# A new step list for a windowed attention with four experts behind it, on one core

## The chip, the cores and the metric

The kernel runs on one NeuronCore of a Trainium2 chip. The metric is device time in microseconds of one launch, as the median of several runs. Five runs of the kernel before lie between 232.1 and 235.28 us, with a median of 234.81 us.

## The reference

Inputs are q, k and v of shape (8 batches, 8 heads, 576 positions, 64), and weights of a gate (512 x 4), of four experts' projections (4 x 512 x 64 each for q, k and v) and of their outputs (4 x 64 x 512). All are float32. Cut to what is computed:

```python
scores = (q @ k.T) / 8, where |i - j| <= 32, else -1e9   # per batch and head
x = softmax(scores) @ v            # heads joined: (8, 576, 512)
logits = x @ w_gate                # 4 experts; the two largest are softmaxed to weights w
for e in range(4):
    qe, ke, ve = x @ wq[e], x @ wk[e], x @ wv[e]
    ye = causal_softmax(qe @ ke.T / 8) @ ve @ wo[e]
    out += w[:, e] * ye            # 0 for an expert that was not chosen
```

## The kernel before, in words

The program is straight-line code without loops at run time: 901 steps, one after another, as the string ORDER (lines 24 to 89) names them. Each name is an operation, its indices, and, behind an @, the PSUM banks and sometimes the engine. `ex0110@0` is operation ex for batch 0, head group 1, half 1, pair 0, from the bank pair that begins at 0; `xf10@6a` is operation xf for batch 1, part 0, bank 6, on ACT (a; v is DVE, g is POOL). The loop at line 680 calls the functions of these names. Each engine executes its own instructions in the order of this list; semaphores order engines against one another, only where tiles overlap. [...] a step cannot write a bank until whoever reads its former content is through. So the list sets the order on every engine, in SP's queue of transfers, and the use of every bank.

Per batch the steps are these.

- **Loads**: lq and lk bring q and k of four heads (576 KB each), lv brings V in pieces of 128 positions (256 KB; the last is 128 KB); fk and fq are the first batch's loads in halves; wl0 to wl3 bring the weights (512 KB each). All are issued by SP through `load`.
- **First attention**: tq and tk (gq and gk in the first batch) transpose 32 x 32 blocks on DVE. sc writes scores of four heads and half the positions to two bank pairs: 80 loads of weights and 80 matmuls in float32. ex takes their exponential on ACT into A, two steps for each sc. mk multiplies A by the window mask on POOL. vc copies V to make a second alignment. av multiplies A with V (32 matmuls; column 65 is the sum). un divides on DVE into XN.
- **Middle**: xt transposes XN on TensorE, xf copies it out of PSUM, xb casts it to bfloat16. ga computes the gate's logits, and gt, ge, gm, gu make weights of them on DVE and ACT. cw0 to cw3 cast the experts' weights, once.
- **Experts**: pp and pv project (8 matmuls, and 16 or 8), pe and ve copy these out, ps writes scores in four pieces, xe takes exponentials into ATE, se masks on POOL, po multiplies with V (30 matmuls), oe normalises and weights, ox transposes by DMA (pt and ot on TensorE in the last batch), py multiplies by WO, ye copies to Y and st stores it (pz, yz and sz in the last batch).

The steps that begin with s_ prepare constants; s_wm issues 30 matmuls on zeros while the first loads are under way.

Two mechanisms matter here. A load waits for the last TensorE instruction that stands before it in the list, in addition to what its buffer needs:

```python
ins = nc.sync.dma_start(o, i)
if PACE[0] is not None:
    tc.add_manual_dep(ins.ins, PACE[0].ins.name, AFTER, reason="pace")
```

So loads start where TensorE has got to, and SP's queue is in order: a load or store that waits holds those behind it. And the instructions of TensorE themselves come from memory, in blocks, while the program runs; the profile shows them as a queue of their own.

ORDER was written by a search (simulated annealing) that works on a model of the engines; the model isn't part of the kernel. One of its numbers is the time from the request of a block of TensorE instructions to its arrival.

## Time and profile before

| | us |
|---|---|
| median of five runs (lowest, highest) | 234.81 (232.1, 235.28) |
| profiled execution, whole | 236.81 |
| profiled execution, span from first to last instruction | 235.1 |
| TensorE: matmuls busy | 214.9 |
| TensorE: weight loads busy | 174.9 |
| DVE, ACT, POOL busy | 177.5, 155.2, 148.8 |
| mean granted TensorE clock | 0.955 |

In the profile PE is TensorE's matmuls, PEld its loads of weights, DVE is VectorE, ACT is ScalarE, POOL is GpSimd, SP is SyncE. Nearly all instructions carry the line of one helper (line 145), so they are told apart by tiles: "PS<-Tqn,Tkn" is a score step (sc), "PS<-V,A" an av step, "A<-PS" on ACT an ex, "A<-A,MASKP" on POOL a mk. The page divides the span into 40 slices of 5.9 us; its clock row gives tenths of full speed. The chain is the work that ended last, followed back; "issue" is time in which an engine waited for nothing that the profile shows. A median of 277 ns for one matmul is its length in a pipeline, not the distance to the next.

### The profile page before, as it was taken

How to read it: one execution, taken by the hardware profiler on the slowest of the kernel's cores; microseconds unless marked ns; L12 is line 12 of the kernel's file. 1: busy time of each engine (PE TensorE's matmuls, PEld its weight loads, DVE VectorE, ACT ScalarE, POOL GpSimd, SP SyncE). 2: the span in 40 equal slices, each digit the busy share in tenths (PEclk: the TensorE clock that was granted, in tenths of full speed). 3: DMA queues.
4: the chain of work that ended last, by engine and by line, in shares of the span. 5: the costliest groups of instructions: out<-in, count | busy, mean ns of one | idle time of the engine just before them, and what ended most of it. 6: DMA issues, size and time to landing. Idle time of an engine off the chain costs nothing.

```text
span 235.1 us, 12226 instructions
## 1 busy us (share of the span) xinstructions
PE 214.9 (91%) x5485; PEld 174.9 (74%) x5496; DVE 177.5 (75%) x359; ACT 155.2 (66%) x241; POOL 148.8 (63%) x166
## 2 busy tenths in 40 slices
PE   6777799989989989999999899999989999999992
PEld 5656697878779867877876788787888887876650
DVE  7987669987789858978985798877877926665571
ACT  2143319778873867638766767778836788886972
POOL 7089705979971989888699682587820898150220
PEclk9775569999999999999999999999999999999999
DMA  6989467958994589675739788887752554228346
GB/s 177 361 220 321 140 166 177 236 110 229 233 323 129 129 163 228 172 228 122 178 74 322 240 199 167 233 216 121 203 190 105 31 139 162 53 53 231 117 178 230
DMA packets 64533, 42.94 MB, mean 183 GB/s; under 512 B 54752, under 2 KB 55776, under 8 KB 64480
## 3 DMA queue, kind: packets, MB, share of 16 engines
q1 hardware_dynamic: 64400, 42.09, 67.7%
q8 instruction: 43, 0.70, 1.3%
q14 instruction: 10, 0.08, 0.1%
q10 hardware_dynamic: 80, 0.07, 0.1%
HBM read 30.42 MB, written 9.44 MB: 170 GB/s over the span
## 4 chain that ended last, share of the span: by engine, by line
PE 68%; DVE 11%; DMA 7%; issue 6%; ACT 5%; SPq 0%; ACTq 0%; DVEq 0%
PE PS L145 68%; DMA kn<-in_k_dram 5%; DVE Tkn L145 5%; ACT ATE L145 2%; DMA V<-in_v_dram 2%; DVE Tqn L145 1%; ACT V L145 1%; DVE OE L145 1%; DVE PS L145 1%; ACT A L145 1%; DVE XTF L145 1%; DVE VE L145 0%; ACT QKE L145 0%; DVE m L145 0%; ACT Y L145 0%
## 5 line engine op out<-in xcount | busy, mean ns | idle before, releaser
L145 POOL TENSOR_TENSOR A<-A,MASKP 128x576 f32<-128x576 f32 x64 | 89.4, 1417 | 20.6 <-ACT A L145 20.0
L145 ACT ACTIVATE A<-PS 128x576 f32<-128x576 f32 x64 | 38.6, 651 | 40.5 <-PE PS L145 40.3
L145 ACT ACTIVATE ATE<-PS 128x1024 bf16<-128x1024 f32 (+1 forms) x64 | 50.9, 837 | 15.5 <-PE PS L145 14.9
L145 PE MATMUL PS<-Tqn,Tkn 32*64 32x128 f32 (+2 forms) x2560 | 46.6, 277 | 7.5 <-issue 3.8
L145 PEld LDWEIGHTS PS<-Tqn,Tkn 32*64 32x64 f32 x2560 | 41.3, 141 | 13.4 <-issue 5.2
L145 PE MATMUL PS<-V,A 128*64 128x65 f32 (+1 forms) x1280 | 43.1, 234 | 3.0 <-issue 1.9
L145 PEld LDWEIGHTS PS<-V,A 128*64 128x64 f32 (+1 forms) x1280 | 39.5, 142 | 6.9 <-issue 4.1
L145 POOL TENSOR_SCALAR_AFFINE_SELECT ATE<-ATE 128x512 bf16<-128x512 bf16 (+1 forms) x48 | 24.3, 519 | 30.9 <-ACT ATE L145 30.6
L145 DVE STREAM_TRANSPOSE Tqn<-qn 128x576 f32<-128x576 f32 (+1 forms) x34 | 37.4, 1177 | 4.7 <-PE PS L145 2.5
L145 DVE STREAM_TRANSPOSE Tkn<-kn 128x576 f32<-128x576 f32 (+1 forms) x34 | 37.4, 1176 | 3.0 <-DMA kn<-in_k_dram 2.5
L145 DVE TENSOR_TENSOR XN<-PS,RC 128x512 f32<-128x512 f32 (+1 forms) x40 | 25.5, 638 | 1.4
L145 POOL CAST XTB<-XTF 128x128 bf16<-128x128 f32 (+1 forms) x20 | 13.9, 713 | 19.4 <-ACT XTF L145 12.5
L145 POOL COPY V<-V 64x1024 f32<-64x1024 f32 (+1 forms) x20 | 18.6, 931 | 4.1 <-DMA V<-in_v_dram 3.0
L145 PE MATMUL PS<-WO,OTT 128*128 128x512 bf16 (+1 forms) x85 | 18.8, 342 | 0.9 <-DVE G L145 0.3
L145 PE MATMUL PS<-ident,XN 128*128 128x128 f32 x144 | 19.0, 276 | 0.0
L145 PE MATMUL PS<-WV,XTB 128*128 128x256 bf16 (+1 forms) x192 | 18.5, 255 | 0.0
L145 PE MATMUL PS<-XTB,WQ 128*128 128x288 bf16 x128 | 18.2, 286 | 0.1
L145 PEld LDWEIGHTS <-ATE 128*128 128x128 bf16 x480 | 16.7, 97 | 2.1 <-issue 0.8
L145 PE MATMUL PS<-XTB,WK 128*128 128x288 bf16 x128 | 18.2, 286 | 0.0
L145 PE MATMUL PS<-QKE 64*128 64x64 bf16 (+4 forms) x192 | 16.7, 277 | 1.2 <-DVE QKE L145 0.9
L145 PE MATMUL PS<-VE,ATE 128*128 128x65 bf16 x480 | 17.4, 193 | 0.1
L145 PEld LDWEIGHTS PS<-ident,XN 128*128 128x128 f32 x144 | 16.0, 140 | 2.0 <-ACT ATE L145 0.2
(66 smaller groups left out, 241.2 us busy)
## 6 DMA issues: line engine op xcount, KB each, us to landing
qn<-in_q_dram SPq DMA_DIRECT2D x15, 576.0 KB, 5.6
kn<-in_k_dram SPq DMA_DIRECT2D x15, 576.0 KB, 5.3
V<-in_v_dram SPq DMA_DIRECT2D x32, 256.0 KB, 4.4
out_dram<-Y SPq DMA_DIRECT2D x14, 512.0 KB, 3.8
V<-in_v_dram SPq DMA_DIRECT2D x8, 128.0 KB, 3.6
out_dram<-Y SPq DMA_DIRECT2D x4, 256.0 KB, 2.7
out_dram<-YS SPq DMA_DIRECT2D x15, 64.0 KB, 2.8
kn<-in_k_dram SPq DMA_DIRECT2D x2, 288.0 KB, 4.0
```

The lines of the kernel that those rows point to most:

```text
L145: return lambda *a, **k: self._w.note(self._e, f(*a, **k))
```

## The change

Only the string ORDER is new. The search was run anew with a longer assumed time from the request to the arrival of each block of TensorE instructions. The new list has the same 901 step names. What differs is their order, the banks, and for some copies the engine. The beginning and the last steps, before (-) and after (+):

```diff
-    s_mask s_onev s_warm s_onep s_padx s_ident fk01 s_padv@v fq00 fk00 fq01 fq10 gk01 fk10 lq10 gq00 s_wm
-    gk00 lv03 gq01 sc000@02 ex0001@2 mk0001 gq10 lv02 sc001@46 gk10 lk10 lv01 ex0011@6 sc011@62 lv04 lv00
-    tq10 tk10 ex0111@2 mk0011 lq11 s_pada@v vc01@g ex0000@0 sc010@20 tq11 mk0111 mk0000 ex0010@4 mk0010
-    ex0110@6 mk0110 ex0100@2 lq20 lk11 sc101@64 ex0101@0 av02@0 ex1010@6 ex1011@4 vc00@a mk0101 mk0100 lk21
-    av03@6 un02@0 un03@6 wl0 av04@2 un04@2 mk1011 mk1010 av01@0 un01@0 av00@6 un00@6 lk20 sc100@24 wl1
-    ex1001@4 xt00@6 xf00@6a tk11 xt01@0 xt02@4 xf02@4a xf01@0a xb01@a sc111@64 ex1111@4 lv12 lv14 cw0@v tq20
+    s_padx s_onep fk00 fq00 gk00 s_mask fq01 fk01 fq10 fk10 lq10 gq00 s_wm gq01 gk01 lv03 gq10 sc001@02 lk10
+    sc000@46 gk10 lv04 s_warm ex0000@4 ex0010@0 ex0011@2 lv02 sc011@04 tq10 lv01 lq11 tk10 ex0111@4 sc010@24
+    lv00 ex0110@0 ex0001@6 mk0011 vc01@a ex0100@2 ex0101@4 lk11 s_pada@v s_onev tq11 sc101@60 mk0010
+    s_padv@g mk0000 mk0111 lq20 mk0110 av02@4 ex1011@0 lv12 sc100@02 un02@4 lv13 vc00@a mk0101 mk0001
+    s_ident mk0100 av03@4 lk20 ex1001@2 ex1010@6 ex1000@0 mk1011 mk1010 vc11@g tk11 un03@4 av00@0 un00@0 wl1
+    av01@6 xt01@0 xf01@0a wl0 av04@2 un01@6 xt00@6 un04@2 xt02@0 xf02@0v xb01@g xf00@6a xb00@a sc110@24
...
-    oe702@2 pt702@2 ot712@0a yz71@1a sz71 pz70@3 yz70@3a sz70 ot702@2v pz73@2 yz73@2a sz73 pz72@0 yz72@0v
-    sz72 py72@1 ye72@1a st72
+    pt702@0 oe712@6 ot702@0v pz71@1 yz71@1a sz71 pt712@2 pz70@3 yz70@3a sz70 ot712@2v pz72@2 yz72@2a sz72
+    pz73@0 yz73@0a sz73 py72@1 ye72@1a st72
```

Engines of copies that change: cw0, cw2 and cw3 go from DVE to ACT (cw1 stays on DVE); s_padv goes from DVE to POOL; of vc1 ACT has one in place of three, POOL seven in place of five, and of vc0 two and six in place of three and five; two xf0, one pe, two ye2 and one yz go from DVE to ACT; one ve0, one ve1 and one ot go from ACT to DVE, and one ye0. In the new list lv73 stands ahead of pv41, in the old one ahead of mk7001; lv74 stands behind st22, st32 and st20.

## The prediction

> **What bounds the kernel now.** I read the page's busy row and slices first, then the chain that ended last, then the waits, then stretches of 3.41 us at the start, because the clock row is low there.

> ```profile
> PE 214.9 (91%) x5485; PEld 174.9 (74%) x5496; DVE 177.5 (75%) x359; ACT 155.2 (66%) x241; POOL 148.8 (63%) x166
> ...
> PEclk9775569999999999999999999999999999999999
> DMA  6989467958994589675739788887752554228346
> ...
> q8 instruction: 43, 0.70, 1.3%
> ...
> PE 68%; DVE 11%; DMA 7%; issue 6%; ACT 5%; SPq 0%; ACTq 0%; DVEq 0%
> ```

> TensorE bounds: busy for 91%, and 68% of the chain. What can be won is its idle time and its slow clock. Nothing on the chain beside it exceeds 11%. The chain in order of time shows where TensorE stands still for nothing that another engine did:

> ```profile
> 18.79 1.46 issue
> 20.25 5.07 PE PS L145 x103
> 25.32 1.46 issue
> ...
> 82.43 0.62 issue
> ...
> 101.17 0.49 issue
> ...
> 128.77 1.07 issue
> ...
> 174.64 0.70 issue
> ```

> These are instruction fetch. The q8 row has 43 packets of 16 KB (0.70 MB); TensorE's 11,020 instructions are 43 blocks of 256. Numbered in the trace, the stalls stand before instructions 705, 961, 4033, 5057, 6080, 6591 and 8892: all within five of a multiple of 256 less 63. Each of them ends about 1.4 to 1.65 us after the end of a q8 packet (18.61 to 20.25; 25.28 to 26.79; 81.66 to 83.05; 128.42 to 129.84). With 0.43 before 119.5 TensorE's gaps there are 1.46 + 1.46 + 0.62 + 0.48 + 0.43 + 1.07 + 0.70 = 6.2 us. [...] the packet for 961 started 4.15 us after the block before it had begun to execute.

> The stretches, with busy time of PE, PEld, DVE, ACT, POOL, then clock, DMA share and GB/s:

> ```profile
> 9.29:12.71 3.42, 3.42 (x144) 3.36 (x142) 3.42 (x4) 0.65 (x1) 0.97 (x1) 0.50 0.93 294
> 12.71:16.12 3.41, 1.91 (x89) 1.34 (x82) 3.11 (x3) 1.41 (x3) 2.83 (x3) 1.00 0.85 227
> 16.12:19.53 3.41, 2.67 (x80) 2.22 (x81) 2.54 (x3) 2.26 (x5) 3.35 (x4) 0.50 1.05 230
> 19.53:22.95 3.42, 2.69 (x89) 2.47 (x89) 1.92 (x4) 0.94 (x2) 3.42 (x4) 0.50 1.01 363
> 22.95:26.36 3.41, 2.37 (x43) 2.19 (x42) 3.01 (x4) 2.82 (x4) 3.41 (x3) 0.50 0.56 185
> 26.36:29.77 3.41, 2.98 (x65) 2.69 (x66) 1.50 (x4) 0.00 (x0) 1.46 (x2) 0.50 0.39 122
> 29.77:33.19 3.42, 3.42 (x82) 3.30 (x86) 1.40 (x4) 0.00 (x0) 0.00 (x0) 0.50 0.69 158
> 33.19:36.60 3.41, 3.36 (x90) 2.92 (x74) 3.41 (x6) 2.01 (x5) 0.01 (x1) 1.00 0.80 218
> ```

> The clock halves and returns in steps of one stretch. It returned only after stretches with TensorE busy throughout (3.42 of 3.42), and one with 2.98 of 3.41 (87%) did not bring it back. The two long fetch stalls lie in stretches that therefore stayed at half: from 16.12 to 33.19 us TensorE is at half speed. A score step (sc) takes 2.31 us there against a median of 1.30 over all, an av step 1.68 against 0.93: 0.56 of the speed, so a stretch at half clock costs 3.41 x 0.44 = **1.5 us**.

> [...]

> **The change part by part.** All 901 steps stay, so TensorE runs the same 10,992 loads and matmuls. Order, banks and the engine of some copies move.

> (a) **Head, to the first score step at 8.62**: no change, 0. The four half loads stand in another order, but both lists need all four before the first scores, and DVE's last two pairs of transposes follow the last landing as before (6.77 to 9.11). s_padv goes from DVE (1.14 us from 3.00) to POOL; this work ends before 4.2 and the landing at 6.74 hides it. Were the cover gone it is 1.1.

> (b) **First exponentials.** Before, sc011 waits for two ACT steps of which one was early (12.94 to 13.64). After, the first ACT steps are ex0000@4, ex0010@0, ex0011@2, and sc011@04 needs the first two: two of 0.65 after the second score step, so +0.66. The first mask step follows the third ACT step, 14.95 instead of 11.74. Before av02, POOL then has mk0011, mk0010, s_padv, mk0000, mk0111, mk0110: 14.95 + 5 x 1.42 + about 1.0 (DVE's time for s_padv is 1.14 and POOL's is not shown; bounds 0.5 and 2.0) = 23.05. vc01 goes to ACT, where 2 x 0.94 is hidden, as ACT idles 40.5 us before such steps. So av02 starts at **23.1 against 22.46**, +0.6, whatever the fetch before it does.

> (c) **Fetch in the head.** By the fifth score step the old list has issued 3,456 KB of q, k and v since s_wm, the new one 2,880 KB (lq20 now follows sc101, lv00 sc010). Block 705, at the start of sc101 (2.2 us there), came at 20.25 and may come as late as 20.8 without delaying av02: its stall lies beside (b)'s mask wait and costs nothing more. Block 961 now lies early in sc100, about 25.2[...]. I take its 1.46 as gone (bounds 0 and 1.46 left). The old list spends 13.77 us from av02 to sc111 (36.23); the new list does the same steps (sc100 earlier) in 12.3 without the stall: 23.1 + 12.3 = 35.4. (b) and (c) together: **-0.8**.

> (d) **Clock.** From 23.1 on the new list has sc100, av03, av00, xt01, av01 behind one another with masks done by 28.05 for av00, which starts about 28.7. A stretch at full clock one earlier is 1.5, two 3.0, none 0. I take one: **-1.5**.

> (e) **Fetch after 36 us**: 3.3 us now. With the steps laid end to end at the trace's median of each kind (sc 1.30, av 0.93, pp 0.97, ga 1.22, pv 1.87), 13 blocks of the old list last under 3.6 us, 8 of the new[...]. What goes is half or less: **-1.3**, bounds 0 and -3.3. When a stall goes, what is late next is an ACT copy out of PSUM: the old waits there are 0.3 to 1.0 us each.

> (f) **Copies and SP's queue**: cw0, cw2 and cw3 go from DVE (0.8 + 0.7 + 1.9) to ACT, one vc0 and two vc1 from ACT to POOL (1.9 each); some xf, pe, ve, ye and yz swap. DVE is on the chain from 33.5 to 47.6, but TensorE lost little there (0.83 at av12): 0, bounds -0.8 and +0.8; the cover is over 55 us idle on each of these engines. Near the end the old chain runs through a V load issued at 190.8 (lv73, 3.76 us) and ACT's copies of it to 199.4; TensorE lost 0.43 at ps612 after them. The new list issues lv73 some 40 us earlier and copies on POOL: **-0.4**, bounds 0 and -0.8. In its place lv74 now stands behind three stores (st22, st32, st20) in SP's order, each waiting for its copy; 128 KB that vc70 and av74 need some 20 us later, so 0.

> (g) **Tail**: yz72 moves to ACT, which then has four copies of 0.58 and ye72 of 0.37 in a row. ACT ended at 231.0; now 231.3. **+0.3**. The gate chain gt7 to gu7 keeps its place behind ga7.

> Sum: -0.8 - 1.5 - 1.3 - 0.4 + 0.3 = -3.7. The profiled execution took 236.81 us (span 235.1, 1.7 around it), 2.0 above the median of the runs, 234.81, whose five lie between 232.1 and 235.28. That spread is about what one or two stretches of clock make, so part of (d) is already in the median: I count 1.0 of 1.5. That leaves -3.2: 234.81 - 3.2 = **231.6 us**.

> **Rivals.** *The stalls only move* (the change does not do what it says). For it: [...] chains of short blocks near the fourth to eighth boundary with 1,600 KB beside them. Against it: less load ahead of 961. Then (c) and (d) give nothing, (b) costs 0.6, (e) 0.5 instead of 1.3 and (f) and (g) cancel: 234.81 + 0.6 - 0.5 = 234.9.

> *Slower: the clock stays at half because of the mask wait.* With sc011 late by 0.66 and the wait before av02, TensorE is idle more in the stretches from 12.7 to 23. If block 961 comes over 0.45 us late (13% of a stretch, the idle share that kept the clock low at 26.36), the stretch that follows av02 stays slow and so does the next. Price: two stretches, 3.0, with 0.6 of (b) and 0.3 of (g), less 0.5 of (e): 234.81 + 3.4 = 238.2. From 0.45 us on it decides. Against it: the old list already loses nearly the same stretches, so there is little left to lose beyond one more.

> **How the numbers follow.** Forecast 0.5 (its own range 228.8 to 233; a tenth of it lies within 1%), stalls only move 0.30, slower 0.20. A measurement here cannot tell under about 1% (2.3 us). Faster by over 1% (under 232.5) is 0.9 of the forecast, 0.45; slower (over 237.2) is most of the last rival and a little of the second, 0.19; the rest 0.36. Range 228.6 (a second stretch of 1.5 and half as much again of (e), some 1.5 in all beyond it: 231.6 - 3.0) to 237.3, which leaves half of the slower case out.

> **What would show it.** Right: av02 near 23, no gap before instruction 961, full clock from 26.4 or 29.8, chain pieces "issue" of over 0.4 us summing to under 3.5 against 6.2. Wrong: gaps of a microsecond at other block boundaries, half clock beyond 33, or new TensorE waits for ACT or POOL of over 1 us.

## The result

The new list takes 232.56 us (median of 44 runs, 229.04 to 237.76) against 233.85 us for the old one (79 runs, 230.41 to 239.13). The ratio is 0.9949, with a 95% interval of 0.9924 to 0.9973: faster by half a per cent, which lies inside the 1% that I had called no difference. Two later series put the same pair at 0.9992 (0.9960 to 1.0025) and 0.9922 (0.9885 to 0.9959). The ratios leave disturbed executions out; some of the profiled executions below lie 2 to 5 us above the median of their kernel, so spans of single profiles are not compared as times.

The page of the new list: its busy row, the clock and the chain by engine.

```profile
span 229.8 us, 12210 instructions
...
PE 211.4 (92%) x5485; PEld 170.5 (74%) x5496; DVE 172.4 (75%) x348; ACT 152.2 (66%) x240; POOL 154.2 (67%) x178
...
PEclk9976999999999999999999999999999999999999
...
PE 79%; DVE 6%; DMA 5%; ACT 4%; issue 2%; SPq 1%; ACTq 0%; DVEq 0%
```

Set beside the page of before, this looks like the forecast come true: "issue" falls from 6% of the chain to 2%, the low part of the clock row shrinks, and the span by 5.3 us. The chain in order of time (start, duration) has these pieces of "issue" over 0.4 us; the first three are TensorE before instructions 4033, 4545 and 5312, in place of seven such gaps that made 6.2 us:

```profile
79.02 0.56 issue
89.80 0.62 issue
103.59 0.45 issue
184.97 0.52 issue
```

But a second profile of the *old* list (experiment 1) has the clock row of the new one, and its span is 230.2 us. Its page, and the pieces of its chain that are block boundaries (449, 1217, 1985, 4033, 6080):

```profile
span 230.2 us, 12226 instructions
...
PEclk9976999999999999999999999999999999999999
```

```profile
13.60 1.01 issue
28.63 0.82 issue
42.18 0.63 issue
79.25 0.90 issue
115.52 0.47 issue
```

And a second and a third profile of the *new* list have long stalls again (from the chain of the third; 449, 1985, 4033, 4545):

```profile
14.33 0.77 issue
44.61 1.23 issue
...
82.88 1.10 issue
93.95 1.72 issue
```

So the profile that I argued from had a slower start than any later profile of the old list, and the profile after has the fewest late blocks of the three of the new list. Two tables of these five profiles show what repeats. The first is about gaps, stretches of over 0.15 us in which TensorE does nothing. A fetch gap is one that stands at a block boundary (within ten instructions of a multiple of 256 less 63) and that no other engine or load ended, so far as the profile shows. The other gaps are counted from the first score step to the end.

| profile | execution, us | fetch gaps before 45 us | after 45 us | other gaps | half clock, us |
|---|---|---|---|---|---|
| old, first | 236.81 | 2.9 | 3.6 | 4.0 | 20.5 |
| old, second | 231.97 | 3.0 | 2.0 | 5.2 | 6.8 |
| new, first | 231.79 | 0.4 | 1.6 | 7.3 | 6.8 |
| new, second | 234.25 | 2.3 | 4.6 | 5.4 | 6.8 |
| new, third | 236.40 | 2.7 | 3.3 | 6.0 | 13.7 |

The two executions of nearly the same time, the second of the old list and the first of the new one, differ by 3.0 us in fetch gaps, and by 2.1 the other way in the other gaps.

The second table gives how far the program is behind a list without any wait. The steps of the list are laid end to end, each with the median duration of its kind; a step that then starts at x us really starts later, and the table has the difference.

| behind by, us, at x = | 30 | 50 | 60 | 90 | 160 | 190 |
|---|---|---|---|---|---|---|
| old, first | 15.3 | 17.1 | 18.2 | 21.2 | 24.6 | 24.7 |
| old, second | 12.3 | 13.6 | 14.9 | 17.7 | 19.8 | 19.7 |
| new, first | 12.2 | 14.0 | 14.0 | 18.1 | 18.4 | 19.4 |
| new, second | 12.8 | 15.1 | 15.1 | 21.3 | 21.6 | 22.2 |
| new, third | 15.3 | 17.9 | 17.9 | 23.5 | 23.7 | 24.3 |

In the head, the first 33 us or so, there is no gain: where both lists have done the same TensorE steps (before sc111 in the old, before sc110 in the new), the second old profile stands at 32.68 us and the first two new ones at 32.72 and 32.82. From 90 to 160 the old list loses 3.4 and 2.1 us and the new one 0.3, 0.3 and 0.2. From 60 to 90 it is the other way round: 3.0 and 2.8 against 4.1, 6.2 and 5.6. The change cleaned one stretch of the program and made another worse.

The gaps say with what. From 90 to 160 the old list has fetch gaps of 2.2 and 0.7 us and no other gap of over 0.15, and the new one has no gap of over 0.15 at all, in any of its three profiles. From 60 to 90 the fetch gaps are 1.4 and 1.2 us in the old list and 1.6, 4.1 and 2.8 in the new one. So late blocks went from the later stretch to the earlier one. They make up only a part of what the old list loses from 90 to 160; the rest, 1.2 and 1.4 us, lies in no gap of over 0.15 and stays unexplained.

### The profile page after: what moved, and what is told of

Same layout as the page of the kernel before. It is cut to its first block, busy times and chain, and to the rows that moved or that the text cites. A ratio compares the mean times of both kernels' runs of the same rounds, so it can differ in the third digit from the quotient of the medians.

```text
span 229.8 us, 12210 instructions
## 1 busy us (share of the span) xinstructions
PE 211.4 (92%) x5485; PEld 170.5 (74%) x5496; DVE 172.4 (75%) x348; ACT 152.2 (66%) x240; POOL 154.2 (67%) x178
## 4 chain that ended last, share of the span: by engine, by line
PE 79%; DVE 6%; DMA 5%; ACT 4%; issue 2%; SPq 1%; ACTq 0%; DVEq 0%
PE PS L145 79%; DMA qn<-in_q_dram 3%; DMA V<-in_v_dram 2%; DVE Tkn L145 1%; ACT A L145 1%; DVE Tqn L145 1%; ACT V L145 1%; SPq L365 1%; DVE PS L145 1%; DVE QKE L145 1%; ACT XTB L145 0%; ACT XTF L145 0%; DVE m L145 0%; ACT ATE L145 0%; DVE OE L145 0%
## 5 line engine op out<-in xcount | busy, mean ns | idle before, releaser
L145 POOL TENSOR_TENSOR A<-A,MASKP 128x576 f32<-128x576 f32 x64 | 89.5, 1419 | 22.8 <-ACT A L145 22.8
L145 ACT ACTIVATE ATE<-PS 128x1024 bf16<-128x1024 f32 (+1 forms) x64 | 50.3, 838 | 15.5 <-PE PS L145 15.0
L145 ACT ACTIVATE A<-PS 128x576 f32<-128x576 f32 x64 | 38.1, 650 | 27.7 <-PE PS L145 27.6
L145 PE MATMUL PS<-Tqn,Tkn 32*64 32x128 f32 (+2 forms) x2560 | 46.3, 270 | 4.2 <-DVE Tkn L145 2.0
L145 PEld LDWEIGHTS PS<-Tqn,Tkn 32*64 32x64 f32 x2560 | 40.1, 136 | 10.7 <-issue 5.3
L145 POOL TENSOR_SCALAR_AFFINE_SELECT ATE<-ATE 128x512 bf16<-128x512 bf16 (+1 forms) x48 | 23.9, 518 | 29.1 <-ACT ATE L145 29.0
L145 DVE STREAM_TRANSPOSE Tkn<-kn 128x576 f32<-128x576 f32 (+1 forms) x34 | 37.2, 1177 | 7.1 <-DMA kn<-in_k_dram 6.0
L145 PE MATMUL PS<-V,A 128*64 128x65 f32 (+1 forms) x1280 | 39.8, 223 | 2.9 <-ACT A L145 1.9
L145 PEld LDWEIGHTS PS<-V,A 128*64 128x64 f32 (+1 forms) x1280 | 36.2, 132 | 6.3 <-ACT A L145 2.2
L145 DVE STREAM_TRANSPOSE Tqn<-qn 128x576 f32<-128x576 f32 (+1 forms) x34 | 37.2, 1179 | 2.1 <-DMA qn<-in_q_dram 1.3
L145 POOL COPY V<-V 64x1024 f32<-64x1024 f32 (+1 forms) x26 | 24.0, 923 | 5.0 <-DMA V<-in_v_dram 2.7
L145 DVE TENSOR_TENSOR XN<-PS,RC 128x512 f32<-128x512 f32 (+1 forms) x40 | 25.5, 638 | 1.5
L145 ACT COPY XTF<-PS 128x1024 f32<-128x1024 f32 (+1 forms) x24 | 16.2, 709 | 6.7 <-PE PS L145 6.6
L145 PE MATMUL PS<-XTB,WK 128*128 128x288 bf16 x128 | 18.0, 286 | 1.9 <-DVE G L145 1.1
L145 ACT CAST QKE<-PS 128x576 bf16<-128x576 f32 x20 | 12.8, 646 | 10.2 <-PE PS L145 10.2
L145 PE MATMUL PS<-WO,OTT 128*128 128x512 bf16 (+1 forms) x85 | 18.5, 341 | 0.6
L145 PE MATMUL PS<-ident,XN 128*128 128x128 f32 x144 | 18.8, 277 | 0.1
L145 PE MATMUL PS<-WV,XTB 128*128 128x256 bf16 (+1 forms) x192 | 18.7, 256 | 0.1
L145 PE MATMUL PS<-XTB,WQ 128*128 128x288 bf16 x128 | 18.2, 287 | 0.1
L145 PEld LDWEIGHTS <-ATE 128*128 128x128 bf16 x480 | 16.5, 97 | 1.9 <-issue 0.6
L145 POOL CAST XTB<-XTF 128x1024 bf16<-128x1024 f32 (+1 forms) x20 | 12.9, 662 | 7.1 <-ACT XTF L145 6.1
L145 PE MATMUL PS<-VE,ATE 128*128 128x65 bf16 x480 | 17.4, 193 | 0.0
```

Source lines behind the costliest of these rows:

```text
L145: return lambda *a, **k: self._w.note(self._e, f(*a, **k))
```

## The experiments

**1 and 2: both lists once more**, unchanged, for a second profile of each and the clock of many runs.

> The list of before, unchanged, profiled once more and timed against itself. All theories: ratio 1.00 within 0.5%. It says how typical the first profile was, with its 20.5 us at half clock before 33 us and its 6.2 us of fetch stalls. Theory A (the clock in the head makes the spread): runs with a lower mean clock are slower, about 1.5 us for each stretch of 3.41 us at half clock (0.0074 of the mean clock), so a fit over the runs gives near 200 us per unit of clock. Theory B (the clock hardly matters, the spread is waits and fetch): below 100 us per unit.

> The new list, unchanged, profiled once more, timed beside the old one. All theories: ratio near 0.995. The profile tells whether 1.6 us of fetch stalls (0.55, 0.62, 0.45) is typical of the new list: theory A and B both expect under 3 us, against 4 to 6 in the old list.

Measured: 1.0033 (0.9995 to 1.0070) and 0.9992 (0.9960 to 1.0025) of the old list's own runs. The median of the mean clock is 0.983 for the old list (43 runs) and 0.9835 (22 runs); for the new list it is 0.9815 in the runs of the result and 0.9775 here. The new list does **not** get a higher clock. A straight line through the runs falls by 82 and 112 us per unit of clock in the old list and by 74 and 101 in the new one, with correlations of only -0.34 to -0.37. The runs of experiment 9 give 102 for the old list and 132 for the new one, at -0.50 and -0.41. That is 0.5 to 1.0 us for a stretch of 3.41 us at half clock (0.0074 of the mean). So neither theory quite: the slope is about half of what A needs and around the limit of B, and the clock goes with 12 to 25% of the spread. That the clock is the cause of that part is not shown by such a line. The other expectation failed: the second profile of the new list has 6.9 us of fetch gaps where both theories had under 3, and the old one 5.0.

**3 and 4: the halves**. A list is cut at its 147th step, and all steps that are left follow in the order of the other list. In short (steps are matched by name, and three and two steps at the seam take the bank in which their data already stands):

```diff
-ORDER = old list                        # 3: the first 147 steps of the new list, then the old one's rest
+ORDER = new[:147] + [s for s in old if s not in new[:147]]
-ORDER = old list                        # 4: the reverse
+ORDER = old[:147] + [s for s in new if s not in old[:147]]
```

> The new list up to its 147th step (about 50 us), then all remaining steps in the order of the old list, banks and engines of its own. Forecast of the prediction: the head (its parts b, c, d) brings -1.8 of the -3.2 us, so ratio about 0.993. Rival 'the head is a wash' (the new wait of 1.9 us for ACT before av00 takes back what the fetch saved): ratio 0.999 to 1.001. Rival 'all of it in the head': ratio 0.994 to 0.996 here and 1.000 in the next run.

> The old list up to its 147th step, then all remaining steps in the order of the new list. Forecast of the prediction: part e, f, g bring -1.4 us, ratio about 0.994. Rival 'the head is a wash': all of the gain is here, 0.994 to 0.996. Rival 'all of it in the head': 1.000.

Measured: 1.0291 (1.0213 to 1.0369) and 1.0194 (1.0094 to 1.0294). Neither expectation: both are slower than either parent. The profiles lose 4.7 and 6.1 us between x = 30 and 40, at the seam, in waits of TensorE for DVE and ACT at instructions 2379 to 2537 (up to 1.59 us) and around the first projections. A list is a fit of the whole, and a cut costs more than the difference that was to be split, so the times say nothing about the halves. Behind the seam, from x = 50 to the end of the list, the rest of the old list loses 9.5 us and the rest of the new one 4.9. The two profiles of the old list lose 8.4 and 6.9 there, the three of the new one 5.7, 7.4 and 6.7. From 90 to 160 the rest of the old list again has fetch gaps, 2.0 us, and the rest of the new one none. And the heads, the same as in the parents, again take as long: 31.60 us for the old and 32.26 for the new, at the point compared above. That agrees with a gain in the rest alone.

**5 and 6: every block boundary moved by half a block.** The warm-up on zeros gets 64 matmuls and 64 weight loads more, each much smaller, so that all later instructions stand 128 places further on.

```diff
-        for i in range(30):
-            nc.tensor.matmul(PS[3][:, 1, 288:512], WZ[:, 0:128], WZ, start=True, stop=True)
+        for i in range(94):
+            nc.tensor.matmul(PS[3][0:32, 1, 288:360], WZ[:, 0:32], WZ[:, 0:72], start=True, stop=True)
```

> Old list; the warm-up s_wm has 94 small matmuls (32 x 72) in place of 30 large ones (128 x 224), so every later instruction of TensorE stands 128 places further on, half a block of 256. The warm-up ends before the first scores in either form, or delays them by under 1 us. Theory F (the new list is fitted to where the block boundaries fall): the old list was never fitted well, so it changes little, ratio 0.995 to 1.005. Rival (boundaries are not what the lists differ by): the same.

> New list with the same half-block shift. Theory F: fetch stalls of the fitted list come back, so it loses 1 to 2 us against its own unshifted runs: ratio to the old list 1.002 to 1.008, worse than the shifted old list or equal to it. Rival (boundaries are not what the lists differ by, stalls are met anywhere): ratio 0.993 to 1.000, still ahead of the shifted old list by 0.3 to 0.5%.

Measured: 1.0867 (1.0767 to 1.0967) for the old list and 1.0782 (1.0708 to 1.0856) for the new, some 18 to 20 us. The plain medians of six runs each are 256.74 and 248.96 us. All expectations missed by a wide margin, and this is the largest effect in the study. The chain of the shifted old list, from an execution of 259.51 us:

```profile
10.39 2.04 issue
...
39.71 2.77 issue
57.25 1.47 issue
...
79.49 1.18 issue
87.89 2.35 issue
102.20 2.12 issue
113.34 2.09 issue
129.61 2.33 issue
145.70 2.54 issue
```

Nearly every one is a fetch gap at a boundary before or inside a score step, the step with the densest instructions (160 in a median of 1.30 us). Fetch gaps after 45 us sum to 17.1 us in the old list and 15.0 in the new one, against 1.6 to 4.6 unshifted, and half clock returns in the middle of the program, in six stretches of 3.41 us after 40 us in the old list. The first scores start at 8.01 and 8.43 us, as unshifted, and most of the loss comes later, so the warm-up itself isn't it. **Both** lists do well only with the boundaries where they were, as far as one shift tells. That is what I hadn't thought of: the old list was already made with a time for the fetch, and the new assumption had only a remainder to win. The two intervals overlap; that the new list would bear the shift better is not shown.

**7 and 8: no loads of q, k and v for batches 2 to 7.** Their steps work on the data of batches 0 and 1.

```diff
     def lq(b, g):
-        load_qk("qn", q, b, g)
+        if b < 2:
+            load_qk("qn", q, b, g)
...
     def lv(b, m):
+        if b > 1:
+            return
```

(lk as lq.)

> Old list without the loads of q, k and v for batches 2 to 7 (their steps compute with the data of batches 0 and 1). Theory C (a block of instructions comes late because it waits behind bulk loads): gaps at block boundaries after 45 us sum to under 1 us, against 3.3 and 1.4 in the two profiles of the old list; time falls by 2 to 4 us, ratio 0.983 to 0.991, the rest of it from waits for data. Rival ([...] dense blocks stall anyway): the gaps stay above 1.5 us and the ratio above 0.993.

> New list without the same loads. Theory C together with my forecast (the new list gains by keeping loads off the fetches): it has less to win from this than the old list, so the two without loads are equal within 0.3%. Rival (the new list gains in the waits between engines, fetch stalls are as many in both): the new list without loads stays ahead by 0.5 to 1%.

Measured: 226.47 us, 0.9818 (0.9760 to 0.9876), and 225.62 us, 0.9783 (0.9726 to 0.9840). Theory C holds: after 45 us not one fetch gap of over 0.15 us is left in either list, though the lists and the blocks are the same. In what way the loads delay the packets these runs do not show. The waits of TensorE's weight loads on PS that the profile puts down to nothing, in the new list without the late loads and, in its third profile, with them (us, times, longest):

```profile
PEld PS L147 <- issue: 5.7, 25, 0.5
```

```profile
PEld PS L145 <- issue: 12.2, 30, 2.0
```

What is left are waits of 0.5 at most. By the ratio the late loads cost the old list 1.8%, some 4.2 us, waits for their data among it. For the second question, whether the lists are then equal, the answer is between the two expectations: the new list is ahead by 0.36%, 0.85 us, with intervals that overlap. From x = 90 to 160 the old list still loses 1.0 us without the loads and the new one 0.2; with them it was 2.1 to 3.4 against 0.2 to 0.3. So in that stretch more of the gain goes with the loads than without them. The 0.8 us that stays lies in no gap of over 0.15 us in either list, and what it is stays open.

**9 and 10: one load out of a burst.** In its second and third profile the new list stops for 1.72 us before instruction 4545, in the gate of batch 2 (ga2); in the first it stops there for 0.62, with the same loads about it. SP's queue there, in the third profile (start, duration, transfer), and the end of that wait in TensorE's weight loads:

```profile
81.49 3.74 SPq L626 DMA_TRANSPOSE OTT<-OE  x2
85.87 1.83 SPq L234 DMA_DIRECT2D V<-in_v_dram  x2
87.89 2.09 SPq L234 DMA_DIRECT2D kn<-in_k_dram  x2
```

```profile
95.67 0.14 PEld L145 LDWEIGHTS PS<-XTF,WG 128*32 128x32 f32 x2 [2.04 <-issue]
```

SP is held by the two transposing transfers ox00 and ox01, and behind them four loads of 1,664 KB together go out within about 4 us (lv43, lv41, lk41, lk50). The block before 4545 began at 87.99; the packet for 4545 started at 93.30, 5.3 us later, and TensorE went on 1.4 us after it had landed. The edit moves one load:

```diff
-    ... pe200@6v lk50 tk40 ...
+    ... pe200@6v tk40 ... av34@6 gt2@7 un34@6 lk50 lv54 lv52 ...
```

> The new list again, beside the old one and beside three variants of it: a third profile and the reference of this call. Ratio 0.995 to 1.000. Fetch stalls at instructions 4033, 4545 and 5312 as in its first two profiles (0.55 and 1.10, 0.62 and 1.72, 0.45 and 0.99 us), each time with loads that were released together just before.

> New list, with one load of 576 KB (lk50) moved from behind pe200 to behind un34. There it no longer stands in the burst of four loads that SP releases after the two transposing transfers ox00 and ox01, while the block for instruction 4545 is fetched. Theory C (the block waits behind the burst): the gap before 4545 (0.62 and 1.72 us before) falls under 0.5; the time falls by about 0.5 us, ratio 0.998 to the new list, hardly measurable. Rival (the fetch is late for another reason, the transposing transfers or the block's own length): the gap stays.

Measured: 0.9922 (0.9885 to 0.9959) for the new list and 0.9874 (0.9793 to 0.9955) with the load moved, an interval too wide to rank the two, and the plain medians (231.27 of 19 runs, 233.94 of 6) even stand the other way round. The trace is clear, however. With one load of kn less in the burst the gap is gone (the same two views; the last line is the gap before 5057, of which more below):

```profile
77.26 2.91 SPq L628 DMA_TRANSPOSE OTT<-OE  x2
80.89 1.41 SPq L236 DMA_DIRECT2D V<-in_v_dram  x2
82.91 0.34 SPq L236 DMA_DIRECT2D kn<-in_k_dram  x1
```

```profile
87.94 1.22 PEld L147 LDWEIGHTS PS<-XTF,WG 128*32 128x32 f32 x32 [0.21 <-issue]
...
98.64 0.92 PEld L147 LDWEIGHTS PS<-Tqn,Tkn 32*64 32x64 f32 x57 [1.15 <-issue]
```

The packet starts 3.4 us after the block before it, not 5.3, and in run 12 with the same edit also 3.4. Two more profiles have this part of the new list with the load unmoved, and stop at 4545 too: run 4 for 0.90 us and run 11 for 1.63. So five profiles without the edit have the gap and two with it have none, though the transposing transfers and the blocks are the same. Theory C holds for a single stall. But in both edited runs a gap of 0.93 us appears two blocks on, before instruction 5057, where the moved load now goes out. None of the five unmoved profiles has a gap there. A stall was moved: 0.93 us in place of 0.62 to 1.72.

**11 and 12: the head of the new list.** In the new list TensorE waits before av03 for DVE (un02 stands behind the transposes of tq11, which wait for their load) and before av00 for ACT (ex1000 stands behind the copies of vc00, which wait for lv00). Its weight loads in the first profile, with the wait in brackets:

```profile
24.58 1.01 PEld L145 LDWEIGHTS PS<-V,A 128*64 128x64 f32 x32 [0.75 <-DVE XN L145]
27.63 1.95 PEld L145 LDWEIGHTS PS<-V,A 128*64 128x64 f32 x64 [2.04 <-ACT A L145]
```

```diff
-    ... lv01 lq11 tk10 ex0111@4 sc010@24 lv00 ... s_onev tq11 sc101@60 ... sc100@02 un02@4 ... ex1001@2 ex1010@6 ex1000@0
+    ... lv01 lv00 lq11 tk10 ex0111@4 sc010@24 ... s_onev sc101@60 ... ex1011@0 ex1010@6 ... un02@4 tq11 ... ex1000@0 ex1001@2
```

> New list with four steps of the first 30 us moved: the load lv00 ahead of lq11, the transposes tq11 behind un02 on DVE, ex1010 behind ex1011 and ex1000 ahead of ex1001 on ACT. Theory H (the new list's head loses what it saved in waits before av03 and av00): the waits there, 0.6 to 0.9 us for DVE and 1.0 to 1.9 us for ACT, go; 1 to 2 us less, ratio to the new list 0.992 to 0.997. Rival (the head is bound by the landing of q and k and by the masks, so another wait follows at once): within 0.2%.

> Both edits. If they add: 1.5 to 2.5 us less than the new list, ratio to the old list 0.985 to 0.992, faster than either list. Rival: no better than the new list, within 0.3%.

Measured: 1.0004 (0.9972 to 1.0035) of the old list with the head reordered, slower than the new list beside it, and 0.9962 (0.9923 to 1.0002) with both edits. Theory H falls, in a way worth seeing. Both waits are gone, and in their place, in run 11:

```profile
18.61 1.98 PEld L147 LDWEIGHTS PS<-Tqn,Tkn 32*64 32x64 f32 x79 [1.21 <-issue]
...
24.91 1.50 PEld L147 LDWEIGHTS PS<-Tqn,Tkn 32*64 32x64 f32 x64 [2.37 <-issue]
```

These are blocks 705 and 961 (gaps of 1.02 and 2.13 us; block 961 is late by 2.12 in run 12 too): with lv00 ahead of lq11 three loads go out behind sc011, 1,088 KB, ahead of these two blocks. TensorE's waits of 1.9 to 2.5 us in the three profiles of the new list were bought off with 3.2 us of fetch. TensorE also waits 1.8 us for DVE before the first projections in both runs, against 0.7 in the new list; run 3, whose head is that of the new list, has the same 1.8, so it is not put down to the edit. No list here beats the new one for certain.

## Why the prediction was right and wrong

The direction was right, and the range held the time; the size was wrong. I said 231.6 us, -3.2; the ratio makes it -1.2. The range, 228.6 to 237.3, also holds no change at all, so that it held says little. The rival that the stalls only move, at 234.9, described the mechanism better than my forecast did: a stall at 4545 and a longer one at 4033 in place of those at 5057, 6080 and 6591. Two of my own signs of being wrong came: a wait of 1.90 us for ACT (before av00), and gaps of over a microsecond at the boundaries 1985, 4033 and 4545 in the second and third profile. The slower rival did not come in the times: the new list's masks begin earlier, and its median clock is lower by 0.006 at most. Something like it shows in the third profile alone, where TensorE is busy for 1.34 us of 3.41 around the wait for ACT before av00 and a stretch at half clock follows, from 28.68.

- **(a) nothing before the first scores**: right; they start at 8.20 in the new list and 8.01 in the second old profile.
- **(b) av02 0.6 later**: wrong in sign. av02 starts at 20.76 in the new list, 21.57 in the second old profile. I counted the exponentials from 12.9, when the second score step ended in a stretch at half clock. At full clock ACT had done the first three by 12.69, so the masks began 2.1 us sooner. The wait that came was elsewhere: 0.6 and 1.9 us before av03 and av00, which I had taken as free.
- **(c) the stall at 961, -1.46**: that loads make the block late holds (experiments 7 to 12; with 1,088 KB ahead of it the gap was 2.13 and 2.12 us in 11 and 12), but the stall is 0.58 in the second old profile and 0.24, 0.32 and 0.46 in the new ones. That it would go altogether was my estimate of the room that the fetch has; when a block is requested is not shown in the profile. With (b), **-0.8 measured as 0**.
- **(d) a stretch of clock, -1.0 in the median**: this is the step that failed most. The median clock doesn't rise, so there is nothing to count; and by the lines through the runs a stretch goes with 0.5 to 1.0 us, not 1.5. I took the 17 us at half clock of one profile for the usual state, while its time, 236.81, already stood 2.0 us above the median. Nor does full clock need a stretch with TensorE busy throughout, as I read it: in the first new profile it returns at 21.44 after a stretch busy for 3.06 us of 3.41.
- **(e) later stalls, -1.3**: not shown in the sums, 3.6 and 2.0 us against 1.6, 4.6 and 3.3. (My 3.3 for the first profile left out a gap of 0.30 before 4289, and that half or less would go was no more than my estimate.) It holds from x = 90 to 160, where fetch gaps of 2.2 and 0.7 us are gone, and is lost again from 60 to 90 at the burst.
- **(f) the V load near the end, -0.4**: wrong. From x = 160 to 190 the old list loses 0.1 and -0.1 us, the new one 1.0, 0.6 and 0.6. The piece of the chain through DMA and ACT was real, but TensorE hardly waited for it.
- **(g) the tail, +0.3**: about right; from the last weight load to the end it takes 4.8 and 4.9 us in the old list, 5.2, 4.9 and 5.0 in the new one.

What remains is half a per cent, and x = 90 to 160 is where it shows. How much of it is fetch is not settled: in the whole program the second and third profile of the new list have 6.9 and 6.0 us of fetch gaps against 6.5 and 5.0 in the old one, and without late loads the new list keeps a lead of 0.36%, which these runs can't tell from nothing or from all.

## What to carry to other kernels

Before arguing from a stall in a profile, take a second profile of the same kernel: gaps at instruction fetch and the clock at the start varied here by more than the change was worth (2.0 to 6.9 us of fetch gaps and 6.8 to 20.5 us at half clock in five profiles, against 1.2 us). In a straight-line program whose TensorE is the bound, number its instructions: the gaps that stood here at multiples of 256 less 63 were late blocks. The one at 4545, of 0.62 to 1.72 us, was mended by releasing one load less around the time at which the block before begins, and a load that is moved must be followed to the next boundary. And any edit that adds or removes TensorE instructions early on moves all later boundaries: these two lists, tuned to them, lost 8.7 and 7.8% by that alone, far more than the edit between them is worth.

## What the runs showed of the hardware that I had not expected

```profile
93.51:96.92 3.41, 1.69 (x38) 0.91 (x29) 2.32 (x2) 1.47 (x3) 0.22 (x1) 1.00 0.12 39
96.92:100.33 3.41, 3.41 (x78) 3.23 (x78) 1.47 (x4) 1.29 (x4) 0.00 (x0) 0.50 0.72 153
```

The second profile had the same gap of 1.72 us, from 91.41 to 93.13, without half clock, and the first profile of the new list has TensorE busy for 1.51 of 3.41 us from 24.86 to 28.27 and stays at full clock. Busy time in such a stretch alone does not decide, then; what does is not shown.
